# Reordering the opening of a fused FFT, MLP and gate kernel: forward products for 1024 tokens ahead of the first backward block

## The chip, the core and the metric

The kernel runs on one core of one Trainium2 chip. The metric is the device time of one execution in microseconds (us). A core has five engines with instruction streams of their own: PE (TensorE, matrix products and transposes), DVE (VectorE), ACT (ScalarE), POOL (GpSimd) and SP (SyncE). Here SP and POOL mostly issue DMA transfers, and PE's weight loads are shown as PEld.

## What is computed

With S = 2048 tokens, D = 1024 and F = 3584, all inputs bf16:

```python
x = A_x
g = sigmoid((x * gate_w).sum(-1, keepdims=True))
a = irfft2(rfft2(x) * (w_r + 1j * w_i))          # over tokens and columns
r = relu(x @ w1 + b1)
b = (r * r) @ w2 + b2
out = g * a + (1 - g) * b
# and the gradients of A_x, w_r, w_i, w1, b1, w2, b2, gate_w for grad_out
```

The kernel gives `out` and all eight gradients; `B_x` is not used, since the MLP's input is x too. For the MLP's hidden layer the kernel needs two products per token and hidden column: the forward one, h = x w1, and the backward one, d = db w2^T, where db = (1 - g) grad_out. Together they give r and dh = 2 d r.

## The kernel before

**What lies where.** `xT` and `dbT` are x and db transposed, D on the partitions, so that both products contract over D. A "row tile" is 128 tokens; there are 16. `turn_x(i)` and `turn_grad(i)` (L1747 to L1757) turn one row tile with eight 128x128 transposes on PE (`turn_tile`, L661 to L666) and copy the result from PSUM to `xT` or `dbT`: for x mostly on ACT, for gradients mostly on DVE. `gate_of` (L678) makes the gate's sum of a row tile on DVE, `gate` (L683 to L690) the sigmoids of four row tiles on ACT, and scales four row tiles of the gradient (`dbn`) by 1 - g on DVE.

**The products.** Hidden columns come in blocks of 128, in pairs fp = 0, 1, ...; tokens in four blocks of 512, s = 0 to 3. `forth(fp, s, c)` (L819) makes one forward product, block c of pair fp for tokens s: eight 128x512 matmuls into a PSUM bank "ph" (L776), relu on ACT into `rT` (L777), and after the pair's second block the square on ACT into `h2T` (L751), which POOL stores. `back_(fp, s, c)` (`grads`, L779 to L790) makes one backward product: eight matmuls into another bank "pd" (L783) from `w2T`, then one DVE instruction (L787) that writes `dhT` = 2 d r; after four of them POOL stores the wide `dhT` tile. At first ph and pd share two banks; there are three `rT` buffers, two wide `dhT` buffers and two `w2T` buffers. `load_w2` (L792) fills one `w2T` buffer, four column blocks (512 columns) wide, in two halves, each one transposing DMA on SP's queue.

**The order around the change.** The order on each engine is mostly that in which the program issues its instructions; a tie (`after(...)`) fixes it where the scheduler would choose otherwise, `later["last"]` being the newest L787 instruction and `later["newest"]` the newest forward matmul. `mlp_in` is a generator: each `next(units)` makes one step. Its opening (L957 to L981) makes column pairs 0 and 1 for all tokens: for each s, four forward products and then four backward ones, the last four backward products (s = 3) being left waiting for the units that follow. The driver (L1766 to L1838) puts between these steps the loads of x and gradient rows, the turns, the gate, the stores of `dbn` to `db_scr`, and the first stage of the FFT (`first_stage`: DVE instructions that fold rows, matmuls `pk` at L293 and `pu` at L325, stores of `z_scr`). The first two half products (`half_hidden`, L758) use row tiles 0 and 1 while 2 and 3 are turned.

After the opening come units that make the forward product of four blocks (two column blocks by two token halves of 1024) with seven half-size products in place of eight, Strassen's way (L884). They need sums of quadrants of x (`x_sums`, L852 to L860, DVE, written over `dbn`) and of w1 (`w_sums`, L865 to L873, into `Sw`). The first matmuls of the first unit (`pZ`, `ph<-xT,w1f`) need no sum; the first that does is written `ph<-dbn,Sw` in the profile.

Of the kernel before, what the change touches and what calls it, by code (L numbers as in the profile page):

```python
# [10 lines left out]
P = 128  # L11
BF16 = mybir.dt.bfloat16
FP16 = mybir.dt.float16
FP32 = mybir.dt.float32
ALU = mybir.AluOpType
# [126 lines left out]
def kernel(  # L142
# [22 lines left out]
    nc = tc.nc  # L165
# [7 lines left out]
    S2, DC, FC = g.S2, g.DC, g.FC  # L173
    R1, R2 = g.R1, g.R2
    NT = S // P
    Q, H, LW, W1 = D // 4, D // 2, g.Df + 1, g.Df
    NH = D // H
    FGW, FG, FGC = g.FGW, g.FG, g.FGC
# [5 lines left out]
    ld, st = nc.sync.dma_start, nc.gpsimd.dma_start  # L184
# [4 lines left out]
    cten = {k: nc.inline_tensor(v, name=f"c_{k}") for k, v in consts.items()}  # L189
# [11 lines left out]
    pers, _ = pool("pers", stack=ctx)  # L201
# [48 lines left out]
    def after(ins, earlier, wait=mybir.DependencyClass.Sync):  # L250

        if earlier is not None:
            info = mybir.DependencyInfo(wait, mybir.DependencyReason.DATA)
            tc.add_manual_dep(ins.ins, earlier.ins.name, info, reason="paced")
# [406 lines left out]
    def turn_tile(dst, i, src, copy):  # L661

        pt = tps.tile([P, DC, P], BF16, name="pt", tag="tr", bufs=2)
        for b in range(DC):
            nc.tensor.transpose(pt[:, b, :], src[:, b * P : (b + 1) * P], identb[:])
        return copy(out=dst[:, :, of_tile(i)], in_=pt[:])  # L666

    def vectors(vrow):
# [9 lines left out]
    def gate_of(i, row, earlier):  # L678
        w_, product = later["gate"]
        summed = STT(out=product, in0=row, scalar=1.0, in1=w_, op0=ALU.mult, op1=ALU.mult, accum_out=pgs[:, i : i + 1])  # L680
        after(summed, earlier, mybir.DependencyClass.NoSync)

    def gate(i0):  # L683

        c_ = slice(i0, i0 + 4)
        pg = pgs[:, c_]
        nc.scalar.activation(omg[:, c_], pg, ACT.Sigmoid, scale=-1.0)
        nc.scalar.activation(gcol[:, c_], pg, ACT.Sigmoid)
        for i in range(i0, i0 + 4):
            nc.vector.tensor_scalar(out=dbn[:, i, :], in0=dbn[:, i, :], scalar1=omg[:, i : i + 1], scalar2=None, op0=ALU.mult)  # L690

    def ahead_to(n, earlier=None):
        for j in range(len(xs), min(n + 1, NT)):
            xs[j] = f1.tile([P, 2, D], BF16, name="src", tag="src", bufs=3)
            for t in range(2):
                T, i = divmod(2 * j + t, NT)
                after((ld if j < 3 else st)(out=xs[j][:, t, :], in_=(go_perm if T else x_perm)[i]), earlier)
# [28 lines left out]
    def mlp_in():  # L726
# [26 lines left out]
        def new_rT():  # L753
            return wb.tile([P, 2, SW], BF16, name="rT", tag="rT", bufs=3)
# [34 lines left out]
                accum_out=gb1part[:, fc, sb : sb + 1],  # L789
            )  # L790

        def load_w2(fg, earlier=None, halves=(0, FGW // 2)):  # L792

            if fg not in w2T:
                w2T[fg] = wb.tile([P, DC, FGW], BF16, name="w2T", tag="w2T", bufs=2)
            for h in halves:
                f0 = fg * FGW + h
                after(turned(w2T[fg][:, :, h : h + FGW // 2], B_w2[f0 : f0 + FGW // 2, :]), earlier)

# [4 lines left out]
        def load_w1(fp):  # L804
            w1[fp] = f1.tile([P, DC, PW], BF16, name="w1f", tag="w1f") if fp == 2 else wb.tile([P, DC, PW], BF16, name="w1g", tag="w1g", bufs=2)
            ld(out=w1[fp][:], in_=w1v[:, :, fp * PW : (fp + 1) * PW])
# [12 lines left out]
        def forth(fp, s, c, by_rows=False):  # L819
            first, at = (s % 2 == 0, s % 2) if by_rows else (c == 0, c)  # L820
            if first:
                pair[0] = new_rT()
            rT = pair[0][:, at, :]
            hidden(2 * fp + c, rows_(s), w1[fp], rT)
            rTs[fp, s, c] = rT
            if not first:
                out = h2_of(fp, s // 2)
                squared(pair[0][:], out[:, c] if by_rows else out[:, :, s % 2, :])
            if c == 1 and s % 2 == 1:
                store(h2T_scr, h2.pop((fp, s // 2)), fp, s // 2)  # L830
# [34 lines left out]
        def w_sums(fp, tie=None):  # L865
            (a11, a12), (a21, a22) = w_quads(fp)
            if fp % 2:
                s_ = kept[:, NT - 2 : NT, :].rearrange("p t (n f) -> p (t n) f", f=P).rearrange("p (q n) f -> p q n f", q=4)
            else:
                s_ = wb.tile([P, 4, KH, P], FP16, name="Sw", tag="Sw", bufs=1)  # L870
            s1, s2, s3, s4 = (s_[:, n] for n in range(4))
            for out, x, y, op in ((s1, a21, a22, ALU.add), (s2, s1, a11, ALU.subtract), (s3, a11, a21, ALU.subtract), (s4, a12, s2, ALU.subtract)):
                after(V(out=out, in0=x, in1=y, op=op), later["last"] if tie else None, mybir.DependencyClass.NoSync)  # L873
                yield
            S_[fp] = {1: s1, 2: s2, 3: s3, 4: s4}
# [83 lines left out]
        load_w1(1)  # L959
        yield  # L960
        half_hidden(0, 0), half_hidden(1, 0)
        load_w2(0, halves=(0,))
        yield
        load_w2(0, halves=(FGW // 2,))
        yield
        waiting = []
        for s in range(4):
            for what in (forth, back_):
                for fp in range(2):
                    for c in range(2):  # L970
                        if s == 3 and what is back_:
                            waiting.append((fp, s, c))
                        else:
                            what(fp, s, c)
                        if s == 2 and what is forth and fp + c == 0:
                            load_w2(1, later["last"])
                        yield
            if s == 1:
                load_w1(2)
        for _ in w_sums(2, True):  # L980
            pass  # L981
        seq = [(fp, sp) for fp in range(2, LAST - 2) for sp in range(2)]
# [756 lines left out]
    def rows_of_x(k, n=4, lo=0):  # L1739
        for i in range(4 * k + lo, 4 * k + lo + n):  # L1740
            if i % 2 == 0:
                pair = f1.tile([P, 2, D], BF16, name="xsrc", tag="xsrc", bufs=3)
            rows[i] = pair[:, i % 2, :]
            ld(out=rows[i], in_=x_perm[i])

    def rows_of_grad(k, n=4, lo=0):
        for i in range(4 * k + lo, 4 * k + lo + n):  # L1747
            ld(out=dbn[:, i, :], in_=go_perm[i])

    def turn_x(i):  # L1750
        copied = turn_tile(xT, i, rows[i], nc.vector.tensor_copy if i in (1, 3) else nc.scalar.copy)
        if i > 3:
            gate_of(i, rows.pop(i), later["last"])
        return copied

    def turn_grad(i):
        turn_tile(dbT, i, dbn[:, i, :], nc.scalar.copy if i in (1, 3) else nc.vector.tensor_copy)  # L1757
# [16 lines left out]
    vrow = f1.tile([FC + DC, P], BF16, name="vrow", tag="vrow")  # L1774
    nc.scalar.dma_start(out=vrow[FC : FC + DC, :], in_=gate_w.rearrange("(fc p) -> fc p", p=P))
    nc.scalar.dma_start(out=vrow[0:FC, :], in_=B_b1.rearrange("(fc p) -> fc p", p=P))
    next(units)
    rows_of_x(0, 2, 2)
    next(units)
    rows_of_grad(0)  # L1780
    for i in range(2):
        turn_x(i)
# [5 lines left out]
        last_turned = turn_x(i)  # L1788
    for i in range(4):
        gate_of(i, rows.pop(i), last_turned if i else None)  # L1790
    rows_of_x(1)
    next(units)
    stage = None
    for k in range(NT // 4):
        i = 4 * k
        if k + 1 < NT // 4:
            rows_of_grad(k + 1)
        next(units)
        if k:
            turn_grad(i), turn_grad(i + 1)  # L1800
        next(units)
        turn_grad(i + 2) if k else gate(0)
        next(units)
        if k:
            turn_grad(i + 3)
        else:
            for to, name in ((kf, "kf"), (flip, "flip"), (sel, "sel"), (cf, "cf")):
                after(st(out=to[:], in_=cten[name].ap()), later["newest"])
            for n in range(4):
                turn_grad(n)  # L1810
        next(units)
        if stage:
            next(stage)
        next(units)
        if k + 1 < NT // 4:
            turn_x(i + 4), turn_x(i + 5)
        next(units)
        if k + 1 < NT // 4:
            turn_x(i + 6), turn_x(i + 7)
        next(units)  # L1820
        for n in ((), (0,), (4, 8), (12,))[k]:
            after(st(out=db_scr[:, n : n + 4, :], in_=dbn[:, n : n + 4, :]), later["last"])
        if k + 1 < NT // 4:
            gate(4 * (k + 1))
        if k + 2 < NT // 4:
            rows_of_x(k + 2)
        if k == 0:
            ahead_to(1)
            stage = first_stage()
        next(stage)  # L1830
        if k == 3:
            for _ in later["x_sums"](0):
                pass
        next(units)
        next(stage)
    V(out=gpg[:], in0=gcol[:], in1=omg[:], op=ALU.mult)
    later["more_banks"]()

# [79 lines left out]
```

## Time and profile before

| | us |
|---|---|
| time, median of 3 runs | 1198.91 |
| the three runs | 1198.21, 1202.25, 1198.91 |
| the profiled execution's own time | 1203.86 |
| its span, first to last instruction | 1202.1 |
| busy in the span: PE / DVE / ACT / POOL | 1179.5 / 893.5 / 535.8 / 375.9 |
| mean granted PE clock, share of full speed | 0.999 |

The profile is one execution recorded by the hardware. A timeline line gives the start, the time from the first start to the last end, engine, source line, operation, written tile `<-` read tiles, shape and count; in brackets is the idle time before it and what ended it. A line of waits gives the total, the count and the longest. A line of DMA issues gives the queue's engine, the count, the size of one and the median time from issue to landing. A line of a stretch gives its length, then for PE, PEld, DVE, ACT and POOL the busy time and number of instructions, then the granted clock, the DMA share and GB/s.

### The profile page before, as it was taken

To read this page: it belongs to the slowest core of one execution; us is meant where nothing else is said; L and a number is where in the kernel's file an instruction comes from. 1 tells how busy PE (TensorE), PEld (TensorE's weight loads), DVE (VectorE), ACT (ScalarE), POOL (GpSimd) and SP (SyncE) were. 2 spreads that over 40 slices of the span, in tenths; PEclk is the share of its full clock that TensorE was granted. 3 is DMA by queue.
4 is the path that set the end of the run, shared out by engine and by line. 5 is a ranking of instruction groups with operands and counts; after the bars stand their busy time and mean duration, and the time that the engine had idled before them with its cause. 6 is when DMAs were issued, how large, how long until landed. Compare 5 with 4: busy or idle time off the path is not lost.

```text
span 1202.1 us, 19429 instructions
## 1 busy us (share of the span) xinstructions
PE 1179.5 (98%) x7181; PEld 636.1 (53%) x7275; DVE 893.5 (74%) x1598; ACT 535.8 (45%) x961; POOL 375.9 (31%) x618
## 2 busy tenths in 40 slices
PE   8989999999999999999999999999999999999998
PEld 5555555443333444444446899999544444444444
DVE  5878887689898887776637666666786677986757
ACT  5657888576767783444414556564201010000000
POOL 0224433665666663553322322321001100000000
PEclk9999999999999999999999999999999999999999
DMA  9998585686969888989897999994889999665530
GB/s 242 295 237 244 179 210 185 203 200 192 220 189 212 246 243 174 206 183 220 202 225 141 232 218 249 252 208 151 258 170 251 270 255 280 192 188 153 179 123 36
DMA packets 329464, 249.84 MB, mean 208 GB/s; under 512 B 187912, under 2 KB 287658, under 8 KB 328858
## 3 DMA queue, kind: packets, MB, share of 16 engines
q1 hardware_dynamic: 268352, 112.12, 44.8%
q0 software_dynamic: 35136, 111.72, 29.4%
q10 hardware_dynamic: 25882, 24.76, 7.3%
q8 instruction: 57, 0.93, 0.3%
q14 instruction: 37, 0.30, 0.1%
HBM read 114.82 MB, written 89.67 MB: 170 GB/s over the span
## 4 chain that ended last, share of the span: by engine, by line
PE 73%; DVE 12%; DMA 5%; ACT 4%; issue 4%; SPq 1%; POOL 0%; ACTq 0%; another core or an unknown queue 0%; DVEq 0%; POOLq 0%
PE pX L1206 15%; PE xX L1505 13%; PE pV L1206 11%; PE pd L783 8%; PE xV L1505 6%; PE ph L884 6%; PE xZ L1505 3%; DMA dhT_scr<-dhT 1%; PE pui L325 1%; DVE rT L900 1%; PE ph L776 1%; PE pki L591 1%; PE px L435 1%; DVE dhT L787 1%; DMA z<-z_scr 1%
## 5 line engine op out<-in xcount | busy, mean ns | idle before, releaser
L783 PE MATMUL pd<-dbT,w2T 128*128 128x512 bf16 x859 | 205.4, 379 | 4.4 <-DMA w2T<-in_B_w_dram 2.0
L783 PEld LDWEIGHTS <-w2T 128*128 128x128 bf16 x896 | 86.3, 98 | 106.4 <-issue 3.9
L1505 PEld LDWEIGHTS <-dS 128*128 128x128 f16 x686 | 66.3, 98 | 79.1 <-issue 3.4
L787 DVE SCALAR_TENSOR_TENSOR dhT<-pd,rT 128x512 bf16<-128x512 f32 x112 | 76.6, 684 | 32.7 <-PE pd L783 26.0
L1556 POOL DMA_DIRECT2D out_dram<-ot x32 | 17.3, 542 | 249.4 <-DVE ot L1612 128.0
L1622 ACT ACTIVATE w2br<-w2br,dsc 128x512 f32<-128x512 bf16 x8 | 5.8, 722 | 175.0 <-DVE ot L1612 117.4
L1222 ACT COPY u<-pX 128x512 f32<-128x512 f32 x56 | 32.8, 585 | 98.7 <-PE pX L1206 92.6
L1505 PE MATMUL xX<-oT,dS 128*128 128x512 f16 x336 | 76.5, 379 | 0.2 <-DVE eR L1534 0.2
L1505 PEld LDWEIGHTS <-odd 128*128 128x128 bf16 (+1 forms) x462 | 44.8, 98 | 51.5 <-issue 0.9
L1505 PEld LDWEIGHTS <-even 128*128 128x128 bf16 (+1 forms) x448 | 43.6, 98 | 52.6 <-issue 0.7
L1206 PEld LDWEIGHTS <-T 128*128 128x128 f16 x672 | 64.7, 98 | 7.9 <-issue 0.7
L901 ACT ACTIVATE rT<-rT 128x512 bf16<-128x512 bf16 x69 | 43.3, 628 | 40.7 <-DVE rT L900 40.7
L751 ACT ACTIVATE h2T<-rT 128x1024 bf16<-128x1024 bf16 x56 | 59.7, 1065 | 0.5 <-issue 0.2
L1226 DVE TENSOR_TENSOR whi<-pV,u 128x512 bf16<-128x512 f32 x28 | 19.3, 690 | 51.6 <-ACT u L1222 48.1
L475 POOL DMA_DIRECT2D y_scr<-pc x64 | 46.9, 734 | 34.4 <-DVE pc L472 31.9
L446 DVE TENSOR_TENSOR tt<-x,w 128x1028 f16<-128x1028 f16 (+1 forms) x64 | 41.9, 691 | 17.0 <-issue 12.5
L1206 PEld LDWEIGHTS <-S 128*128 128x128 f16 x336 | 32.3, 98 | 41.0 <-DVE S L1138 1.3
L1206 PEld LDWEIGHTS <-resL 128*128 128x128 bf16 x448 | 43.0, 98 | 4.7
L1206 PEld LDWEIGHTS <-resR 128*128 128x128 f16 (+1 forms) x448 | 42.9, 98 | 4.9 <-issue 0.2
L1206 PEld LDWEIGHTS <-even 128*128 128x128 bf16 (+1 forms) x256 | 24.5, 98 | 30.8 <-issue 2.1
L815 POOL DMA_DIRECT2D h2T_scr<-h2T x28 | 20.7, 738 | 62.1 <-ACT f L285 30.8
L499 POOL DMA_DIRECT2D out_dram<-gw x64 | 34.4, 543 | 17.8 <-ACT gw L495 13.9
(381 smaller groups left out, 2757.8 us busy)
## 6 DMA issues: line engine op xcount, KB each, us to landing
h2T_scr<-h2T POOLq DMA_DIRECT2D x28, 512.0 KB, 4.4
dhT_scr<-dhT POOLq DMA_DIRECT2D x28, 512.0 KB, 5.2
y_scr<-pc POOLq DMA_DIRECT2D x64, 128.0 KB, 3.9
ax_scr<-yo POOLq DMA_DIRECT2D x16, 512.0 KB, 5.4
out_dram<-ot POOLq DMA_DIRECT2D x31, 256.0 KB, 3.1
z<-z_scr ACTq DMA_DIRECT2D x60, 128.0 KB, 4.4
out_dram<-whi POOLq DMA_DIRECT2D x28, 256.0 KB, 5.3
out_dram<-wlo POOLq DMA_DIRECT2D x28, 256.0 KB, 5.2
```

Of the source, the lines that this page charges most:

```text
L446: V(out=tt[:, k, :, :, 0:W], in0=x[:, a : a + 2, :, 0:W], in1=by, op=ALU.mult)
L475: st(out=columns_of(y_scr, c, h), in_=pc[:, n])
L499: st(out=every(dst_w, k), in_=gw[lanes[n], c_, 0:W1])
L751: after(nc.scalar.activation(h2T, rT, ACT.Square), behind_, mybir.DependencyClass.NoSync)
L783: mm(pd[:], lhsT=w_[:, ec, fc % FGC * P : (fc % FGC + 1) * P], rhs=dbT[:, ec, ss], start=(ec == 0), stop=(ec == DC - 1),)
L787: return STT(out=dhT, in0=pd[:], scalar=2.0, in1=rT, op0=ALU.mult, op1=ALU.mult, accum_out=gb1part[:, fc, sb : sb + 1],)
L815: st(out=scr[2 * fp : 2 * fp + 2, :, cols2].rearrange("c p s -> p c s"), in_=t_[:])
L884: mm(acc[:], lhsT=lhs[:, t, :], rhs=rhs[:, t, :], start=start and t == 0, stop=t == KH - 1, skip_group_check=True)
L901: nc.scalar.activation(rT, rT, ACT.Relu)
L1206: self.mm = mm(out, lhsT=lhs[:, t, m * P : (m + 1) * P], rhs=rhs[:, t, :], start=start and t + a == 0, stop=t == KH - 1, skip_group_check= ...
L1222: turn["ACT"] = nc.scalar.copy(out=t_[:], in_=self.X[:])
L1505: ins = mm(acc, lhsT=lhs[:, fc, :], rhs=rhs[:, fc, :], start=start and fc == 0, stop=fc == KH - 1 and bias is None, skip_group_check=True,)
```

## The change

1. The opening's order. Before: forward s0, backward s0, forward s1, backward s1, forward s2, backward s2, forward s3. After: forward s0, forward s1, backward s0, forward s2, backward s1, and then by column pair: forward s3 of pair 0, backward s2 of pair 0, forward s3 of pair 1, backward s2 of pair 1. So the opening begins with eight forward products (1024 tokens) and ends with two backward ones, where it ended with four forward ones.
2. Loads. Both halves of `w2T`'s first group are issued in one step, after the loads of x row tiles 6 and 7 and ahead of those of 8 to 11; `w2T`'s second group at the 25th step (tied to the newest L787 instruction then) and no more at the first forward product of s = 2; w1's third pair at the 17th step. Rows of x and of the gradient, and the FFT's constants, are issued at other steps.
3. The driver. The turns of x row tiles 4 to 7 come ahead of any turn of a gradient; the gradient's turns lie beside forward products of s = 1, 2, 3 and backward ones of s = 2; `dbn` row tiles 12 to 15 are stored to `db_scr` after the last step, and `x_sums(0)` is issued after that and after two more FFT steps.
4. Ties. The first transpose of each turn is tied behind the newest forward matmul; the scalings of `dbn` behind the newest L787 instruction; the gate's sums of row tiles from 4 on are no longer required to have such an instruction before them.
5. One `rT` pair, of column pair 1 and s = 1, lies in the buffer "cu" of the later units, since four such pairs are now held at a time.

The diff, its core:

```diff
@@ -662,7 +662,9 @@
 
         pt = tps.tile([P, DC, P], BF16, name="pt", tag="tr", bufs=2)
         for b in range(DC):
-            nc.tensor.transpose(pt[:, b, :], src[:, b * P : (b + 1) * P], identb[:])
+            one = nc.tensor.transpose(pt[:, b, :], src[:, b * P : (b + 1) * P], identb[:])
+            if b == 0:
+                after(one, later.get("newest"), mybir.DependencyClass.NoSync)
         return copy(out=dst[:, :, of_tile(i)], in_=pt[:])
 
     def vectors(vrow):
@@ -687,7 +689,8 @@
         nc.scalar.activation(omg[:, c_], pg, ACT.Sigmoid, scale=-1.0)
         nc.scalar.activation(gcol[:, c_], pg, ACT.Sigmoid)
         for i in range(i0, i0 + 4):
-            nc.vector.tensor_scalar(out=dbn[:, i, :], in0=dbn[:, i, :], scalar1=omg[:, i : i + 1], scalar2=None, op0=ALU.mult)
+            scaled = nc.vector.tensor_scalar(out=dbn[:, i, :], in0=dbn[:, i, :], scalar1=omg[:, i : i + 1], scalar2=None, op0=ALU.mult)
+            after(scaled, later.get("last"), mybir.DependencyClass.NoSync)
 
     def ahead_to(n, earlier=None):
         for j in range(len(xs), min(n + 1, NT)):
@@ -789,11 +792,10 @@
                 accum_out=gb1part[:, fc, sb : sb + 1],
             )
 
-        def load_w2(fg, earlier=None, halves=(0, FGW // 2)):
-
-            if fg not in w2T:
-                w2T[fg] = wb.tile([P, DC, FGW], BF16, name="w2T", tag="w2T", bufs=2)
-            for h in halves:
+        def load_w2(fg, earlier=None):
+
+            w2T[fg] = wb.tile([P, DC, FGW], BF16, name="w2T", tag="w2T", bufs=2)
+            for h in (0, FGW // 2):
                 f0 = fg * FGW + h
                 after(turned(w2T[fg][:, :, h : h + FGW // 2], B_w2[f0 : f0 + FGW // 2, :]), earlier)
 
@@ -819,7 +821,7 @@
         def forth(fp, s, c, by_rows=False):
             first, at = (s % 2 == 0, s % 2) if by_rows else (c == 0, c)
             if first:
-                pair[0] = new_rT()
+                pair[0] = wb.tile([P, 2, SW], BF16, name="rT", tag="cu", bufs=1) if (fp, s) == (1, 1) else new_rT()
             rT = pair[0][:, at, :]
             hidden(2 * fp + c, rows_(s), w1[fp], rT)
             rTs[fp, s, c] = rT
@@ -959,24 +961,20 @@
         load_w1(1)
         yield
         half_hidden(0, 0), half_hidden(1, 0)
-        load_w2(0, halves=(0,))
         yield
-        load_w2(0, halves=(FGW // 2,))
+        load_w2(0)
         yield
-        waiting = []
-        for s in range(4):
-            for what in (forth, back_):
-                for fp in range(2):
-                    for c in range(2):
-                        if s == 3 and what is back_:
-                            waiting.append((fp, s, c))
-                        else:
-                            what(fp, s, c)
-                        if s == 2 and what is forth and fp + c == 0:
-                            load_w2(1, later["last"])
-                        yield
-            if s == 1:
+        steps = lambda what, s, fps=(0, 1): [(what, fp, s, c) for fp in fps for c in range(2)]
+        plan = steps(forth, 0) + steps(forth, 1) + steps(back_, 0) + steps(forth, 2) + steps(back_, 1)
+        plan += [step for fp in range(2) for step in steps(forth, 3, (fp,)) + steps(back_, 2, (fp,))]
+        for n, (what, *step) in enumerate(plan):
+            what(*step)
+            if n == 16:
                 load_w1(2)
+            elif n == 24:
+                load_w2(1, later["last"])
+            yield
+        waiting = [(fp, 3, c) for fp in range(2) for c in range(2)]
         for _ in w_sums(2, True):
             pass
         seq = [(fp, sp) for fp in range(2, LAST - 2) for sp in range(2)]
@@ -1750,7 +1748,7 @@
     def turn_x(i):
         copied = turn_tile(xT, i, rows[i], nc.vector.tensor_copy if i in (1, 3) else nc.scalar.copy)
         if i > 3:
-            gate_of(i, rows.pop(i), later["last"])
+            gate_of(i, rows.pop(i), later.get("last"))
         return copied
 
     def turn_grad(i):
@@ -1774,9 +1772,14 @@
     vrow = f1.tile([FC + DC, P], BF16, name="vrow", tag="vrow")
     nc.scalar.dma_start(out=vrow[FC : FC + DC, :], in_=gate_w.rearrange("(fc p) -> fc p", p=P))
     nc.scalar.dma_start(out=vrow[0:FC, :], in_=B_b1.rearrange("(fc p) -> fc p", p=P))
+    def constants(*names):
+        for to, name in names:
+            after(st(out=to[:], in_=cten[name].ap()), later["newest"])
+
     next(units)
     rows_of_x(0, 2, 2)
     next(units)
+    rows_of_x(1, 2)
     rows_of_grad(0)
     for i in range(2):
         turn_x(i)
@@ -1788,51 +1791,64 @@
         last_turned = turn_x(i)
     for i in range(4):
         gate_of(i, rows.pop(i), last_turned if i else None)
-    rows_of_x(1)
+    rows_of_x(1, 2, 2)
     next(units)
-    stage = None
-    for k in range(NT // 4):
+    next(units)
+    next(units)
+    gate(0)
+    next(units)
+    turn_x(4), turn_x(5)
+    constants((kf, "kf"), (flip, "flip"), (sel, "sel"))
+    next(units)
+    turn_x(6), turn_x(7)
+    for k in range(3):
         i = 4 * k
-        if k + 1 < NT // 4:
+        if k == 0:
+            rows_of_x(2)
+        if k < 2:
             rows_of_grad(k + 1)
         next(units)
-        if k:
-            turn_grad(i), turn_grad(i + 1)
+        turn_grad(i), turn_grad(i + 1)
         next(units)
-        turn_grad(i + 2) if k else gate(0)
+        turn_grad(i + 2)
+        if k == 2:
+            turn_grad(i + 3), gate(12)
+        next(units)
+        if k < 2:
+            turn_grad(i + 3)
+        if k == 0:
+            constants((cf, "cf"))
         next(units)
         if k:
-            turn_grad(i + 3)
-        else:
-            for to, name in ((kf, "kf"), (flip, "flip"), (sel, "sel"), (cf, "cf")):
-                after(st(out=to[:], in_=cten[name].ap()), later["newest"])
-            for n in range(4):
-                turn_grad(n)
-        next(units)
-        if stage:
             next(stage)
         next(units)
-        if k + 1 < NT // 4:
-            turn_x(i + 4), turn_x(i + 5)
+        if k < 2:
+            turn_x(i + 8), turn_x(i + 9)
         next(units)
-        if k + 1 < NT // 4:
-            turn_x(i + 6), turn_x(i + 7)
+        if k < 2:
+            turn_x(i + 10), turn_x(i + 11)
         next(units)
-        for n in ((), (0,), (4, 8), (12,))[k]:
+        for n in ((), (0,), (4, 8))[k]:
             after(st(out=db_scr[:, n : n + 4, :], in_=dbn[:, n : n + 4, :]), later["last"])
-        if k + 1 < NT // 4:
+        if k < 2:
             gate(4 * (k + 1))
-        if k + 2 < NT // 4:
-            rows_of_x(k + 2)
+        else:
+            turn_grad(12), turn_grad(13)
         if k == 0:
-            ahead_to(1)
+            rows_of_x(3), ahead_to(1)
             stage = first_stage()
+        elif k == 1:
+            rows_of_grad(3)
         next(stage)
-        if k == 3:
-            for _ in later["x_sums"](0):
-                pass
         next(units)
+        if k == 2:
+            turn_grad(14), turn_grad(15)
         next(stage)
+    after(st(out=db_scr[:, 12:16, :], in_=dbn[:, 12:16, :]), later["last"])
+    next(stage), next(stage)
+    for _ in later["x_sums"](0):
+        pass
+    next(stage)
     V(out=gpg[:], in0=gcol[:], in1=omg[:], op=ALU.mult)
     later["more_banks"]()
```

## The prediction

> **What bounds the kernel now.** I read the shares of the span first, then TensorE's waits, then the first 95 us engine by engine, because everything the change moves lies there.
>
> ```profile
> PE 1179.5 (98%) x7181; PEld 636.1 (53%) x7275; DVE 893.5 (74%) x1598; ACT 535.8 (45%) x961; POOL 375.9 (31%) x618
> ```
> ```profile
> PE ph L776 <- DVE dhT L787: 3.5, 1, 3.5
> PE pd L783 <- DMA w2T<-in_B_w_dram: 2.0, 1, 2.0
> PE ph L884 <- DVE rT L900: 1.4, 3, 0.5
> ```
>
> PE is busy 98% of 1202.1 us: 22.6 us idle in all. So the time moves only by PE's idle time and its clock. Of these waits the first two lie in the opening. After it PE hardly waits, so whatever the opening loses or gains reaches the end of the span undiminished. The work of PE is the same before and after (7181 matmuls in each program), and from the first `ph<-dbn,Sw` product (89.51 us) on PE's order is the same. I compare the time at which that product can start.
>
> The PE timeline shows both stalls, and what the longer one does to the clock:
>
> ```profile
> 13.59 2.54 PE L776 MATMUL ph<-xT,w1g 128*128 128x512 bf16 x10
> ...
> 27.08 3.63 PE L783 MATMUL pd<-dbT,w2T 128*128 128x512 bf16 x15 [2.00 <-DMA w2T<-in_B_w_dram]
> ...
> 68.53 1.45 PE L783 MATMUL pd<-dbT,w2T 128*128 128x512 bf16 x6
> 73.45 0.64 PE L776 MATMUL ph<-xT,w1g 128*128 128x512 bf16 x2 [3.46 <-DVE dhT L787]
> 73.89 1.16 PE L325 MATMUL pu<-cf,ft 128*128 128x256 f16 x8
> 74.84 2.68 PE L776 MATMUL ph<-xT,w1g 128*128 128x512 bf16 x6
> ...
> 89.51 1.03 PE L884 MATMUL ph<-dbn,Sw 128*128 128x512 f16 x4
> ```
> ```profile
> 20.00:30.00 10.00, 7.76 (x52) 4.26 (x54) 6.97 (x15) 5.74 (x9) 0.00 (x0) 1.00 1.10 232
> 70.00:80.00 10.00, 6.50 (x40) 3.71 (x42) 7.31 (x17) 2.88 (x7) 3.62 (x6) 0.83 1.16 298
> ```
>
> The last three columns of the stretches are granted clock, DMA share and GB/s. After the 3.46 us stall six products take 2.68 us, where six took 1.45 before it, and eight `pu` take 1.16 instead of 0.69 (68.00): 1.2 + 0.5 = **1.7 us lost to the clock**. The 2.00 us stall left the clock at 1.00. [...]
>
> The longer stall comes from VectorE's wait for a store, seen in the DVE timeline and, by its landing, in the DMA issues of 50 to 56 us:
>
> ```profile
> 72.69 0.69 DVE L787 SCALAR_TENSOR_TENSOR dhT<-pd,rT 128x512 bf16<-128x512 f32 x1 [4.02 <-DMA dhT_scr<-dhT]
> ```
> ```profile
> dhT_scr<-dhT POOLq DMA_DIRECT2D x1, 512.0 KB, 17.9
> ...
> z_scr<-u POOLq DMA_DIRECT2D x2, 128.0 KB, 15.7
> w2T<-in_B_w_dram SPq DMA_TRANSPOSE x1, 21.6
> ```
>
> `dhT` has two buffers. The store that frees one was issued at 54.69, behind the start of w2T's second group (SP, 53.26), and landed at 72.57. When the third group is loaded (issues of 100 to 115 us) the same store took 8.4.
>
> **How the profiled run stands to the median.** It took 1203.86, 4.95 above 1198.91. The runs form two pairs, 1198.21 and 1198.91, and 1202.25 and 1203.86. The gap is about this stall with its clock, 3.46 + 1.7 = 5.2. I read the median run as one in which the store landed in time.
>
> **Out goes.** (1) 2.00: both halves of w2T's first group now go to SP right behind the tokens' rows 6 and 7, which wait for the gate sum at 12.84: issued about 13.9. The old halves took 5.19 and 3.12 on the queue; with 10.3 us to land they are there by 24 to 27, and wanted at 30 (four forward products later). (2) 3.46 and 1.7: the `dhT` stores are issued at about 56 to 63, ahead of w2T's second group, which now waits for the `dhT` of the 25th step, about 70; two rows of 8.4 fit. (3) Small waits: PE's groups from 13.59 to 89.51 show 7.2 us idle, 1.7 beyond the two stalls. Sum 2.00 + 3.46 + 1.7 + 1.7 = **8.9**.
>
> **In comes, along the new order.** A product of eight matmuls is 1.73 us (eight by 0.216), a turn of eight transposes 0.44.
>
> *First stall, ScalarE.* From 13.59: two products and four turns of x, 3.46 + 1.78, to 18.83. The next product needs rows 4 to 7 of x, all four turned by ScalarE's copies, and between them stand the relu and the square of the second product. ScalarE can start the relu at 18.15; relu 0.58, copy 0.91, square 0.96, copy 1.01 in their ACT order (rows of 0.67, 1.01, 1.06 with the overlap of neighbours off) end at 21.6. PE waits **2.8**. Nothing is queued ahead of these products on PE that could run. Ends: 1.8 if the square goes behind the last copy (2.8 less 0.96), 2.8 otherwise; I take 2.8, the program's order.
>
> *Middle.* Four forward products with the turns of gradients 0 to 3 (8.7) to 30.3; four backward with four turns to 39.0; four forward, turns and `pk` to 49.5, with 0.9 of small waits on VectorE's copies of dbT and ScalarE's of `ft`; `pu` to 50.0; four backward and turns to 59.2; two forward, `pk`, four turns to 65.0. The next backward product needs dbT of the last of these turns, and VectorE has four `dbn` scalings (1.67, L690) in front: wait **1.1**. Then two backward, two forward, `pk` to 73.3, two backward and so on to 78.2. 0.9 + 1.1 = 2.0. Bounds: 0, since PE's list of old small waits holds 1.7 of the same kind, to 3.5, twice that.
>
> *Last stall, VectorE.* PE has left two turns 0.89, two `pu` 1.06, two `pk` 0.9, the eight first `pZ`/`ph` matmuls 1.73 and one backward product 1.73: at 84.5 it comes to the first `ph<-dbn,Sw`. That needs the sums of x (L859) and w1 (L873). Before, the opening ended with four forward products, whose relu is ScalarE's; VectorE ran ahead:
>
> ```profile
> 79.81 1.22 DVE L859 TENSOR_TENSOR dbn<-xT 128x2048 f16<-128x2048 bf16 x1
> ...
> 85.09 1.22 DVE L859 TENSOR_TENSOR dbn<-xT,dbn 128x2048 f16<-128x2048 bf16 x1
> ...
> 86.31 0.75 DVE L873 TENSOR_TENSOR Sw<-w1f 128x512 f16<-128x512 bf16 x2
> ```
>
> Now it ends with backward products, and VectorE's order has the sums behind the last one's `dhT` (78.4): two dbT copies end at 80.25, then uv and u 0.60 + 0.67 + 0.60, sum 1.14, f 1.21, sum 1.14, f 0.68, sums 2.28, Sw 0.42 and neighbours: 8.7, to 88.9. PE waits 88.9 − 84.5 = **4.4**. The third sum writes `dbn` rows 6 and 7, so it also waits for the store of rows 4 to 7, now issued by POOL at about 76, among the transposes of w2T's second group (about 70). VectorE comes to it at 86.2. Rows: 5.3 and 6.7 for this store, 8.4 and 17.9 for `dhT` among transposes: lands 81 to 94, wait 0 to 7.8. I take **0.5**, nearest to the store's own rows with 8.4 for the neighbours and its double size.
>
> *Clock.* 2.8 stays under the 3.46 that cost something, though above the 2.00 that did not: 0 (to 1.7). [...]
>
> *At nothing:* the tie of each turn on PE and of each scaling on VectorE fix an order and add no instruction; the `rT` of step (1,1) in the "cu" buffer, since "cu" is first written at 86; the later w1 and constant loads on SP (w1f lands long before 79) and POOL (`cf` wanted at 49.5); the store of `dbn` 12 to 15 behind the others, whose reader comes later. If SP is held up by the transposes by the 21.6 above, rows 8 to 15 of x, issued behind them from 21, are the ones late: wanted from 31 on, 10 us later; that costs 0 to 3.
>
> Sum in: 2.8 + 2.0 + 4.4 + 0.5 + 1.7 = **11.4**. Out 8.9. Change against the profile +2.5: 1203.86 + 2.5 = **1206.4**. Against the median, where the 5.2 is already out, it is +7.5, 0.6%. That uses the profile's own time for a run in which nothing of the old stall is left: 1198.7 + 7.7, the same.
>
> **Rivals.** A difference under 0.3%, 3.6 us, cannot be told from none here.
> *The old stall is in the median too* (the 4.95 being only the profiler's): then the net +2.5 stands on 1198.91: 1201.4; without the last clock loss 1199.7. Same. For it: three runs cannot prove two kinds. Against: the two pairs. 0.23.
> *VectorE is in time* (other side): the old stall is in the median, and the sums do not gate PE. Decides from a VectorE that has done Sw by 84.5, 4.4 us earlier than I find, as if the f and u passes (3.8) slid behind the sums. In: 2.8 + 2.0; out 8.9: 1198.91 − 4.1 = 1194.8, faster. Against: VectorE's order is fixed by program and has those passes between. 0.07.
> *The store of dbn is caught* behind w2T's transposes like `dhT` was, 17.9: it lands at 94, the third sum waits 7.8 instead of 0.5: 1206.4 + 7.3 = 1213.7. For it: 17.9, 18.3 and 15.7 among transposes; against: 6.2 for the same store issued at 66 to 69, during the old second half. 0.18. [...]
> *The change does not do what it says*: the order of the PE program shows that it does; 0.
> The forecast, 0.52; its own range, from the ends of the terms, 1203 to 1209.
>
> **Numbers.** Range 1199 to 1212: the first rival and the forecast in it, the store caught only in part, which leaves out some 0.2. Faster 0.07, same 0.23, slower 0.70.
>
> **What would show it.** No wait for w2T near 27, no 3.46 for `dhT`. A PE wait of 2 to 3 us near 19 to 21.6 on ACT xT; one of 4 to 5 near 84 on DVE Sw, with a clock near 0.8 in that 10 us. w2T's second group issued near 70; the store of dbn landing in 5 to 9. Wrong if PE comes to `ph<-dbn,Sw` with the sums done, or if that product starts before 89.

## The result, and the profile after

The changed kernel takes **1205.87 us** (median of 6 runs, 1205.37 to 1206.26). The kernel before, now with 6 runs, has a median of 1197.41 (1195.40 to 1202.25). The ratio is 1.0066, with a 95% interval of 1.0047 to 1.0086: slower by 0.7%. The prediction was 1206.4 in a range of 1199 to 1212, slower with a chance of 0.70. The profiled run took 1205.37 with a span of 1203.5.

From the page of the kernel after, the shares, and below them its longest PE waits (total, times, longest):

```profile
PE 1178.9 (98%) x7182; PEld 636.7 (53%) x7275; DVE 893.2 (74%) x1598; ACT 535.7 (45%) x961; POOL 375.4 (31%) x618
```
```profile
PE ph L886 <- DVE Sw L875: 4.1, 1, 4.1
PE ph L779 <- ACT xT L668: 2.6, 1, 2.6
...
PE pd L786 <- ACT h2T L754: 0.9, 1, 0.9
```

No wait for `w2T` and none for `dhT` is left in the opening; two new ones stand at the top, as forecast. (The added lines shift the numbers: L776, L783, L787, L859 and L884 are now L779, L786, L790, L861 and L886.) The PE timeline has them in their places:

```profile
18.06 1.06 PE L665 MATMUL pt<-identb,xsrc 128*128 128x128 bf16 x16
21.76 1.89 PE L779 MATMUL ph<-xT,w1g 128*128 128x512 bf16 x7 [2.64 <-ACT xT L668]
...
66.19 3.63 PE L786 MATMUL pd<-dbT,w2T 128*128 128x512 bf16 x16 [0.94 <-ACT h2T L754]
...
83.19 1.89 PE L786 MATMUL pd<-dbT,w2T 128*128 128x512 bf16 x8
89.22 1.89 PE L886 MATMUL ph<-dbn,Sw 128*128 128x512 f16 x4 [4.14 <-DVE Sw L875]
90.90 1.13 PE L325 MATMUL pu<-cf,ft 128*128 128x256 f16 x8
```

ScalarE's timeline shows what the first waits for: copy, square, copy in a row, the copy of row tile 7 last.

```profile
18.26 0.69 ACT L780 ACTIVATE rT<-ph,b1col 128x512 bf16<-128x512 f32 x1
18.84 1.00 ACT L668 COPY xT<-pt 128x1024 bf16<-128x1024 bf16 x1
19.73 1.07 ACT L754 ACTIVATE h2T<-rT 128x1024 bf16<-128x1024 bf16 x1
20.69 1.01 ACT L668 COPY xT<-pt 128x1024 bf16<-128x1024 bf16 x1
```

VectorE's shows what the last waits for: the sums begin only at 82.33, and passes of the FFT stand between them.

```profile
78.62 0.69 DVE L790 SCALAR_TENSOR_TENSOR dhT<-pd,rT 128x512 bf16<-128x512 f32 x1 [1.24 <-PE pd L786]
...
82.33 1.21 DVE L861 TENSOR_TENSOR dbn<-xT 128x2048 f16<-128x2048 bf16 x1
83.46 0.68 DVE L277 TENSOR_TENSOR f<-uv 128x1020 f16<-128x1020 f16 x1
...
87.62 1.21 DVE L861 TENSOR_TENSOR dbn<-xT,dbn 128x2048 f16<-128x2048 bf16 x1
88.75 0.74 DVE L875 TENSOR_TENSOR Sw<-w1f 128x512 f16<-128x512 bf16 x2
```

The 0.94 is put down to ScalarE's `h2T`, which ends at 66.18, 0.01 before the product starts at 66.19. VectorE's two dbT copies end at 66.14, 0.05 before it. Elsewhere PE starts about that long after the copy that it waits for (the copy of 20.69 ends at 21.70, its product starts at 21.76). So I read the copies as the cause, and `a_sums` below bears this out: there VectorE's copies end 0.06 before the product and are named. The four scalings of `dbn` end at 63.38 and do not hold these copies up: VectorE waits 0.18 for PE's transposes before it makes them.

```profile
61.65 1.73 DVE L692 TENSOR_SCALAR dbn<-dbn,omg 128x1024 bf16<-128x1024 bf16 x4
63.30 1.28 DVE L668 COPY dbT<-pt 128x1024 bf16<-128x1024 bf16 x2
...
64.85 1.29 DVE L668 COPY dbT<-pt 128x1024 bf16<-128x1024 bf16 x2 [0.18 <-PE pt L665]
```

Around the last wait the clock falls. These are two stretches of the kernel after (the granted clock is the third column from the end), ahead of the wait and with it:

```profile
78.00:84.50 6.50, 6.45 (x64) 4.28 (x65) 5.88 (x11) 4.59 (x11) 2.59 (x6) 1.00 1.04 367
84.50:95.00 10.50, 6.36 (x36) 3.28 (x35) 8.83 (x16) 3.97 (x9) 3.41 (x7) 0.84 0.85 313
```

The four matmuls at 89.22 take 1.89 instead of 1.03 and the `pu` behind them 1.13 instead of 0.68: 1.3 us.

### The profile page after: what moved, and what is told of

It is laid out like the page before. It is cut to its first block, busy times and chain, and to the rows that moved or that the text cites. A ratio compares the mean times of both kernels' runs of the same rounds, so it can differ in the third digit from the quotient of the medians.

```text
span 1203.5 us, 19435 instructions
## 1 busy us (share of the span) xinstructions
PE 1178.9 (98%) x7182; PEld 636.7 (53%) x7275; DVE 893.2 (74%) x1598; ACT 535.7 (45%) x961; POOL 375.4 (31%) x618
## 4 chain that ended last, share of the span: by engine, by line
PE 79%; DVE 11%; ACT 4%; issue 3%; DMA 2%; ACTq 0%; POOL 0%; SPq 0%; DVEq 0%; POOLq 0%
PE pX L1204 15%; PE xX L1503 13%; PE pd L786 12%; PE pV L1204 11%; PE ph L886 7%; PE xV L1503 6%; PE xZ L1503 3%; PE ph L779 2%; PE pui L325 1%; PE px L435 1%; PE pki L591 1%; PE pv L466 1%; PE pu L325 1%; PE pk L293 1%; PE pZ L886 1%
## 5 line engine op out<-in xcount | busy, mean ns | idle before, releaser
L786 PE MATMUL pd<-dbT,w2T 128*128 128x512 bf16 x867 | 206.8, 379 | 2.8 <-ACT h2T L754 0.9
L786 PEld LDWEIGHTS <-w2T 128*128 128x128 bf16 x896 | 86.4, 98 | 105.4 <-issue 3.7
L790 DVE SCALAR_TENSOR_TENSOR dhT<-pd,rT 128x512 bf16<-128x512 f32 x112 | 76.5, 683 | 32.9 <-PE pd L786 32.2
L410 POOL COPY w<-wn 128x512 bf16<-128x512 bf16 x32 | 20.9, 653 | 61.0 <-DVE tt L446 59.8
```

Source lines behind the costliest of these rows:

```text
L786: mm(pd[:], lhsT=w_[:, ec, fc % FGC * P : (fc % FGC + 1) * P], rhs=dbT[:, ec, ss], start=(ec == 0), stop=(ec == DC - 1),)
L790: return STT(out=dhT, in0=pd[:], scalar=2.0, in1=rT, op0=ALU.mult, op1=ALU.mult, accum_out=gb1part[:, fc, sb : sb + 1],)
```

## The experiments

My theory after the result: the changed order costs its own waits, four terms on PE's path (2.64, the small middle ones of 0.94 + 0.42 + 0.31, 4.14, and the clock), and what it takes away is not there in most executions of before. The rivals: the loss is of the loads (moved transposes of w2 and the stores that they delay), or the order as such costs something that no single wait shows. Each kernel ran on a chip together with runs of before; its ratio is to those. Before's median in these jobs was 1196.3 to 1196.9.

### Where before stands: a second profile of it

`b_again` is the kernel before, unchanged.

> The kernel before once more, for a second profile of it. Mine: the 3.46 us wait for dhT belongs to some executions only, those in which the transposes of w2T's second group are slow (dhT store 17.9 us to landing); a run near the median, 1196.3, shows no such wait, a store that lands in 6 to 12 us, and the clock at 1.00. Rival: the wait is in every execution of before, and the 1203.9 of its first profile came from elsewhere.

It took 1196.28, clock 1.00. Neither stall is there. PE's timeline at the two places:

```profile
24.73 3.62 PE L783 MATMUL pd<-dbT,w2T 128*128 128x512 bf16 x16
28.67 1.90 PE L776 MATMUL ph<-xT,w1g 128*128 128x512 bf16 x8 [0.32 <-DVE dhT L787]
...
67.59 0.59 PE L776 MATMUL ph<-xT,w1g 128*128 128x512 bf16 x2
...
81.99 1.03 PE L884 MATMUL ph<-dbn,Sw 128*128 128x512 f16 x4
```

The product of sums starts at 81.99, not at 89.51 as in the first profile: 7.5 us, and the times differ by 1203.86 − 1196.28 = 7.6. So the whole excess of the first profile lies in the opening: 2.00 + 3.46 + 1.7 of clock and some tenths. The store of `dhT` landed in 11.9 here (17.9 there):

```profile
dhT_scr<-dhT POOLq DMA_DIRECT2D x1, 512.0 KB, 11.9
```

Against this profile the changed kernel's product starts 7.2 us later (89.22). Its new waits are 2.64 + 1.67 + 4.14 = 8.45, from which before's own small waits go off, 1.0 by the idle time of its groups in that stretch: 7.45. That is 0.5 more than the 6.9 by which the stretch from the first full forward product (13.71 against 13.39) to that product grew; where the 0.5 goes is not shown. The two runs differ by 9.1 (1205.37 − 1196.28), so behind that product another 1.9 is made: the 1.3 of clock, and 0.6 in what follows, where the kernel after has a PE wait of 0.6 for the load `odd<-h2T_scr` that this profile doesn't show.

### The last wait, by itself

`a_sums` is the changed kernel with the sums of x dealt over VectorE's idle spots, and one store moved forward so that they may be written:

```diff
-        for n in ((), (0,), (4, 8))[k]:
+        for n in ((), (0, 4), (8,))[k]:
...
             turn_grad(i + 3), gate(12)
+            sums = later["x_sums"](0)
+            next(sums)
...
-    for _ in later["x_sums"](0):
-        pass
```

The first changed line is that of the stores of `dbn`; the three other sums follow in later steps of the same turn of the loop.

> The changed kernel, with the four sums of x spread over VectorE's idle spots between 64 and 78 us, and the store of dbn rows 4 to 7 eight steps earlier so that the third sum may write there. Mine: the 4.1 us wait for Sw and the 1.3 us that the halved clock takes after it go, 1205.9 - 5.4 = 1200.5. Rival: the sums delay the dhT evictions that PE waits for, so that half or more of it comes back, 1203 to 1206.

1201.54 (1199.55 to 1204.12), ratio 1.0035 [1.0023, 1.0048], against 1.0066: 3.7 us gained by the ratios, 4.3 by the medians, of the 5.4 that I expected. The wait for Sw is gone (87.18, right behind the backward product of 85.46). But the first sum came between the dbT copies of 64.71 and 67.12, and the wait that those end grew from 0.94 to 1.79:

```profile
21.51 2.84 PE L779 MATMUL ph<-xT,w1g 128*128 128x512 bf16 x7 [2.64 <-ACT xT L668]
24.14 1.81 PE L665 MATMUL pt<-identb,dbn 128*128 128x128 bf16 x16
...
68.46 3.63 PE L786 MATMUL pd<-dbT,w2T 128*128 128x512 bf16 x16 [1.79 <-DVE dbT L668]
...
87.18 1.24 PE L886 MATMUL ph<-dbn,Sw 128*128 128x512 f16 x5
```

Here the product behind the 2.64 us wait runs at the lower clock too: seven matmuls in 2.84, where the kernel after took 1.89, and the 16 transposes 1.81 instead of 1.06, together 1.7 us. The granted clock of 13.6 to 30 us is 0.90 in this profile and 1.00 in that of the kernel after.

### The first wait, by itself

`a_square`: the square that stands between the two copies goes behind the second (`later["square"]` makes the activation of forward step (1, 0, 1), tied behind the copy that it is given).

```diff
-    turn_x(6), turn_x(7)
+    turn_x(6)
+    later["square"](turn_x(7))
```

> The changed kernel, with the square of the second forward pair on ScalarE put behind the copy of x row tile 7. Mine: the 2.6 us wait of PE shrinks by the square's 0.96 and nothing else moves, 1204.9. Rival: the wait is set by another thing than ScalarE's queue (the load of the rows, PSUM), 1205.9.

1204.00 (1203.36 to 1205.80), ratio 1.0058 [1.0043, 1.0073]. The wait is 1.70, 0.94 less:

```profile
20.29 1.89 PE L779 MATMUL ph<-xT,w1g 128*128 128x512 bf16 x7 [1.70 <-ACT xT L668]
```

The ratio moved by 0.0008, 1.0 us (1.9 by the medians), but the two intervals overlap widely; what shows the cause is the wait in the profile, shorter by the square's share. ScalarE's queue sets this wait.

### The clock

`a_fill` puts 16 matmuls of zeros, which nothing reads, into the wait for Sw; `a_fill2` puts 10 more into the first wait. `busy` makes them into a bank of their own.

```diff
             back_(*waiting[0])
+            if not n:
+                busy(16)
             u.p5()
```

> The changed kernel, with 16 matmuls of zeros by zeros, whose result nothing reads, between the first unit's backward product and its first product of sums, so that PE is busy for 3.5 us of the 4.1 us wait for Sw. Mine: the product starts when it did, but at full clock: 1.3 to 2.6 us gained, 1203.3 to 1204.6. Rival: the clock has no part in it, or the added work delays the products, 1205.9 or above.

1203.54 (1202.50 to 1205.72), ratio 1.0048 [1.0031, 1.0065]: 2.3 us by the medians, inside the range given, though the interval still overlaps that of 1.0066. The product starts at the same time as in the kernel after, with PE at full clock:

```profile
84.87 3.62 PE L750 MATMUL pz<-zeros 128*128 128x512 bf16 x16
89.17 1.90 PE L892 MATMUL ph<-dbn,Sw 128*128 128x512 f16 x8 [0.68 <-DVE Sw L881]
90.90 0.68 PE L325 MATMUL pu<-cf,ft 128*128 128x256 f16 x8
```

Eight matmuls now take what four took. The wait itself is no shorter: what is gained is the clock alone.

> The kernel with the zeros in the wait for Sw (a_fill, 1202.5 to 1205.7), and 10 more matmuls of zeros in the 2.6 us wait for ScalarE's copy of x row tile 7, so that PE is idle for 0.5 us there. Mine: the 2.6 us wait halves the clock in some executions (a_fill's slower half); without it all have clock 1.00 and 1202.3 to 1203.3. Rival: a wait of 2.6 us never halves the clock and the spread is the loads': as a_fill.

1202.95 (1202.28 to 1203.03), ratio 1.0051 [1.0039, 1.0064]. The median hardly moves, but the spread closes from 3.2 to 0.75, with a clock of 1.00 in all five runs; in a_fill three of six had 0.998 to 0.999, and those were its three longest. So the 2.6 us wait does cost clock in some executions; `a_sums` shows one.

### The loads of w2T

Five kernels move a load of w2T alone. In `a_w2_16` and `a_w2_20` the second group of the changed kernel is issued earlier; in `b_w2_later` and `b_w2_s1` that of before is issued later and earlier; `b_w2_early` issues both halves of before's first group together. The diffs are of `a_w2_16` (`a_w2_20` has `elif n == 20`), `b_w2_later` (`b_w2_s1` has `s == 1 and what is back_`) and `b_w2_early`.

```diff
-            elif n == 24:
+            if n == 16:
...
-                        if s == 2 and what is forth and fp + c == 0:
+                        if s == 3 and what is forth and fp + c == 0:
...
-        load_w2(0, halves=(0,))
+        load_w2(0)
         yield
-        load_w2(0, halves=(FGW // 2,))
         yield
```

> The changed kernel, with w2T's second group loaded at the 17th step (about 50 us) instead of the 25th (70.6). Mine: the dhT stores of 56 and 63 us fall among the transposes again; where they take 12 to 18 us instead of 3.2 and 6.8, the third dhT tile, wanted at 68.1, waits up to 6 us, so the runs spread from 1205.5 up to 1212, median 1207. Rival: transposes and stores do not get in each other's way, 1205.9 with a spread under 1.

1205.79 (1204.40 to 1207.77), ratio 1.0061 [1.0043, 1.0079]: the rival's time held, though its spread of under 1 did not (3.4). The load went out at 54.23, and transposes and stores landed quickly. This profiled run was the longest of the six (1207.77), and what it has more than the kernel after is mainly clock: 1.35 lost behind the 2.64 us wait and 2.7 behind the wait for Sw.

```profile
dhT_scr<-dhT POOLq DMA_DIRECT2D x2, 512.0 KB, 4.8
...
w2T<-in_B_w_dram SPq DMA_TRANSPOSE x2, 5.3
```

> The changed kernel, with w2T's second group loaded at the 21st step (about 62 us) instead of the 25th (70.6), so that seven transfers of POOL (z, dhT, two src, h2T) are issued while it is transposed, where the 17th and the 25th step met two. Mine: the transposes take 12 to 20 us each and the dhT store of 63.5 lands in 10 to 18 instead of 6.8; the fourth dhT tile, wanted at 75.5, waits up to 6 us in some executions, 1206 to 1212. Rival: the transposes are as quick as at the other two places (4.4 to 7.1) and the time stays at 1205.9.

1206.02 (1203.99 to 1207.33), ratio 1.0074 [1.0061, 1.0088]. The transposes slowed to 10.1 and the store of `dhT` to 8.0, less than I said, and no product waited for it:

```profile
dhT_scr<-dhT POOLq DMA_DIRECT2D x1, 512.0 KB, 8.0
...
w2T<-in_B_w_dram SPq DMA_TRANSPOSE x2, 10.1
```

So the place of this load is worth nothing that can be measured in the changed kernel. The first group was not moved there; but between 13.71 and 89.22 the profile of the kernel after shows no PE wait for a load, and I take the loss not to be of the loads.

> The kernel before, with both halves of w2T's first group issued one behind the other. Mine: the 2.00 us wait at the third backward product goes and nothing replaces it, 1195.4 (2.0 less than before). Rival: the second half now lies ahead of the loads of x row tiles 4 to 7 on SP, and these come late by its 3 to 5 us on the queue; then PE waits for their turns instead, 1197 to 1200.

1196.65 (1195.90 to 1198.04), ratio 0.9993 [0.9981, 1.0004]. The wait for w2T is gone, and in its place PE waits 1.29 for the rows of x that now stand behind the second half on SP, as the rival had it; the median is 1.25 above my 1195.4 and just under the rival's 1197 to 1200:

```profile
20.05 0.62 PE L665 MATMUL pt<-identb,xsrc 128*128 128x128 bf16 x8 [1.29 <-DMA xsrc<-in_A_x_dram]
```

> The kernel before, with w2T's second group loaded at the first forward product of s = 3 and not of s = 2 (some 20 us later, after the dhT stores). Mine: the 3.46 us wait for dhT and its clock loss come from that load and are in some executions of before only; without it no dhT wait is left, the runs close up at the low end of before, 1195.5 to 1197.0 against a median of 1197.4. Rival, the spread of before has another source: the median stays at 1197.4 with runs up to 1202.

1200.08 (1196.04 to 1213.04 in 12 runs), ratio 1.0045 [1.0016, 1.0075]: my expectation failed. There is no `dhT` wait in its profile (1198.51), but half its runs are 1201 to 1213, with a clock down to 0.993. The profile does have a wait of 1.63 for w2T's first group, whose load this kernel leaves as it was.

> The kernel with w2T's second group 20 us later, once more, for a profile of one of its long executions (1204 to 1213), if the draw gives one. Mine: the w1 loads and stores issued behind those transposes land 15 to 20 us late and PE waits for one of them between 85 and 130 us. Rival: the time is lost elsewhere.

This execution was a short one, 1195.35, so what the long ones wait for was not seen. It has no wait for w2T's first group.

> The kernel before, with w2T's second group loaded at the first backward product of s = 1 (about 42 us) and not at the first forward one of s = 2 (51 to 53), ahead of the z, dhT and src transfers. Mine: the transposes take 4 to 8 us each, no execution waits for dhT, and the long executions of before (1198 to 1203) go: median 1195.7, all under 1198. Rival: the long executions have another source, or the later x rows come late behind the transposes on SP: median 1196.5 or more, with a spread as before.

1198.12 (1196.74 to 1199.41), ratio 1.0011 [1.0002, 1.0019]. My expectation (1195.7, all under 1198) failed here too: no `dhT` wait is left, but the median is above before's, and its longest run is level with before's longest beside it (1199.49). Its profiled run was one of its shortest (1196.87), with 0.39 of wait for w2T's first group, and shows no wait that explains the rest.

### The waits together

`a_all` is the changed kernel with the sums dealt out (the first one tied behind the last dbT copy ahead of the wait at 66), the square behind the copy, and 6 matmuls of zeros in what is left of the first wait.

> The changed kernel, with the four sums of x in VectorE's idle spots (the first one behind the last copy of dbT ahead of the wait at 66), dbn rows 4 to 7 stored early, the square of the second pair behind the copy of x row tile 7, and 6 matmuls of zeros in what is left of that wait. Mine: of the four terms of the loss the wait for Sw with its clock (5.4 or more) and 1.0 of the first wait go: 1205.9 - 7.5 = 1198.4, clock 1.00, still 2 above before's 1196.4, which is the first wait's rest of 1.7. Rival: the order as such costs more than these waits, 1200 or more.

1198.67 (1197.50 to 1200.32), ratio 1.0018 [1.0010, 1.0027], clock 1.00 in all runs. By the medians 7.2 of the 8.5 us lost come back, by the ratios 5.7 of 7.9, with the order of the change kept. What its profile still shows of the new waits, the first one's rest of 1.7 (1.3 under the zeros and 0.41) and the 0.94 of the middle, is 2.6, near the 2.2 us that the ratio leaves:

```profile
17.71 1.46 PE L751 MATMUL pz<-zeros 128*128 128x512 bf16 x6
19.57 1.89 PE L787 MATMUL ph<-xT,w1g 128*128 128x512 bf16 x8 [0.41 <-ACT xT L669]
...
64.01 3.63 PE L795 MATMUL pd<-dbT,w2T 128*128 128x512 bf16 x16 [0.94 <-ACT h2T L762]
...
82.74 1.24 PE L899 MATMUL ph<-dbn,Sw 128*128 128x512 f16 x5
```

No version that was run beats before; the nearest, `b_w2_early`, cannot be told from it.

## Why the prediction was right, point by point

- **What bounds the kernel: right.** PE does the same work, and its order is the same from the first product of sums on; from there both kernels need much the same. The 9.1 us between two profiled runs are made in the first 95 us but for 0.6.
- **Out goes, 8.9: right for the profile it was read from, wrong for the median.** All four terms are gone in the profile after. But I took the median execution of before to lack only the `dhT` stall and its clock; the second profile lacks the 2.00 for w2T as well, at 1196.28. That 2.00 is the term that was mis-sized for the median: nothing there could be gained. The wait for w2T's first group comes and goes: in the five profiles in which that load is as before it is 2.00, 1.63, 0.39, 0 and 0. How many executions near the median lack both stalls these do not show.
- **First stall 2.8: right**, 2.64; `a_square` showed ScalarE's queue as the cause by the square's share.
- **Middle 2.0: right in size, not in the cause of its largest part.** It is 0.94 + 0.42 + 0.31 = 1.67. For the largest the forecast had 1.1, from dbT copies held up by the four scalings. The copies are the cause, as putting a sum among them (`a_sums`) lengthened the wait by 0.85. But the scalings were done at 63.38, and the copies waited for PE's transposes: the 0.94 is what the copies take when the product stands right behind its own turns. That 1.1 came out near 0.94 is luck.
- **Last stall 4.4: right**, 4.14, and moving the sums, with the one store that must go ahead of them, removed it.
- **Wait for the store of dbn rows 4 to 7, 0.5: too much.** It landed in 8.3, at about 84.9, and the third sum ran at 86.48 behind the f passes, without a wait. The rival that had it caught (1213.7, 0.18) was open by a margin of 1.6 us. The 6.2 held against it is of the stores issued from 73.69 on, not at 66 to 69.
- **Clock 1.7: right in size**, 1.3 in the profile, about 2.3 by `a_fill`. The term is what the 3.46 us stall cost in the first profile of before; that the expected wait of 4.9 us would cost the same was my estimate, and no run shows it: the wait came out at 4.14, with the 1.3 behind it. The 1.3 is the least that was seen: behind the same wait the slow stretch of `a_square` cost 2.4, those of `a_w2_16` and `a_w2_20` 2.7 (granted clock of 90 to 100 us: 0.69 and 0.68), since there the eight `pk` and the next four matmuls are slow as well. For the 2.64 us wait I took none, with 1.7 as the bound; five profiles of changed kernels hold this wait, and the clock falls in three of them (`a_sums`, `a_w2_16`, `a_w2_20`).
- **The sum.** In came 2.64 + 1.67 + 4.14 + 1.3 = 9.75 in place of 11.4, 1.65 less, and 0.6 came in later waits that I had not seen; so the profiled time moved by 1.5 instead of 2.5. The forecast was for the median, which is 0.5 above the profiled run; the longer executions show the lower clock (0.997 in four of six, 0.999 in the profiled one). So it is partly luck that the median came within 0.5 of 1206.4: 1.65 too much in the sum was offset by the 0.6 and by this 0.5. Against before the loss is 8.5 by the medians where 7.5 was forecast: before's median with six runs is 1.5 lower than the one that was shown.
- **The rivals.** "The old stall is in the median too" fell with `b_again`. "VectorE is in time" fell with the 4.14. What I feared for the stores under the transposes did not happen in the changed kernel at any of three places of the load. That it does what it says was no question: PE's new waits are those of the new order.
- **What stays open.** Why the same transposes land in 5.1, 5.3 and 10.1 us (medians of the two halves in the changed kernel, `a_w2_16` and `a_w2_20`), and in 18.3 in the first profile of before, 14.4 in `b_w2_later`, 13.6 and 14.9 in `b_again` and `b_w2_early` (one half each), but in 9.3 in `b_w2_s1`; what before's long executions (up to 1203.9, with clocks of 0.997 to 0.999 in most of the longer ones) wait for in general, since only one of them was profiled and moving the load that it points to did not shorten the median; what `b_w2_later` waits for at 1213.

## What to carry to other kernels

Where one engine is busy 98% of the span, lay the new order end to end for the engines that feed it as well: the changed opening lost its time because its last products hand their results to VectorE just when VectorE should have made the next operands, and its first ones ask for four copies from ScalarE at once. Take a second profile before counting a stall as something to win: two of the waits in the first one were not in an execution near the median. An idle time of several us on PE can cost more than itself, through the clock (4.14 us and 1.3 more in the kernel after), and matmuls that nobody reads show how much (2.3 by the medians in `a_fill`).

## What the runs showed of the hardware

The clock fell behind a PE wait of 2.64 us in three of five profiles, behind one of 3.46 us in the one that holds it, behind one of 4.1 us in all four that hold it at full length, and not behind those of 1.63, 1.70, 1.79 and 2.00 (one profile each). Where it fell, single stretches lost 1.3 to 2.7 us; the granted clock was 0.50 from 74 to 76 us in the first profile of before and from 89.22 to 91.1 in that of the kernel after. Why the same 2.64 us wait cost clock in three profiles (1.35 in `a_w2_16`, 1.5 in `a_w2_20`, 1.7 in `a_sums`) and none in two, no run here shows.
